# Modulation products with 32 equal moving columns, two more dummies and 48 no-ops, in a fused adaLN attention and MLP kernel

## The chip, the cores and the metric

One core of one Trainium2 chip. The time is the device's time of one execution in microseconds (us), median over the runs given with it; lower is better. Each execution also has a *span*, from its first to its last recorded instruction. The time reaches further: it runs on after the span's end, and "tail" below is the time less the span of the same execution. A ratio of two kernels is the mean time of one kernel's runs over that of the other's of the same rounds, so it is not quite the ratio of the medians.

## The reference

```python
def reference(A_x, A_k_cache, A_v_cache, A_wq, A_wo, B_x, B_w1, B_w2, c, w_mod):
    ...                                     # A: 2048x512, 32 heads of 128, last 512 keys; B: 512-1792-512 with relu
    mod = (_silu(c) @ w_mod).reshape(c.shape[0], 6, 1, -1)
    sa, ca, ga, sb, cb, gb = (mod[:, 0].copy(), ...)
    h = _layernorm(x, axis=-1) * (1 + ca) + sa
    x = x + ga * _A_ref(h, A_k_cache, A_v_cache, A_wq, A_wo)
    h = _layernorm(x, axis=-1) * (1 + cb) + sb
    x = x + gb * _B_ref(h, B_w1, B_w2)
    return x
```

The change touches `sa` and `ca`, the shift and scale of the first normalization: eight column vectors of 128, each a sum of four products of a 128x128 block of `w_mod` with a 128-vector of silu(c).

## The kernel before: the parts that matter

```python
def mm(out_ap, lhsT, rhs, start, stop, reads, bk, signal): ...      # one matmul on TensorE, with waits and signal
def warm(n, gate=(), bk=7):                                          # dummies: 128x512 products of ones, result unused
    for i in range(n):
        mm(bank[bk], ones[:, :], ones[:, 0:1].to_broadcast([P, QB]), True, True, [R_ones] + list(gate), [bk], i == n - 1)

def mod_cols_mm(which, bk):          # 32 products: cc = 4 parts of the weights, each landing by itself; sl, c2 = 8 columns
    ...
    mm(bank[bk][:, col:col + 1], wm[sl][:, cc, c2 * P:(c2 + 1) * P], sc_bf[:, cc:cc + 1], ...)
# [cut]
    ln_tposes(1, TB[0])              # transposes of the normalized rows, 4 per tile
    warm(2, bk=1)
    ln_norm(2)
    mod_half(0, 0, DVE)              # scale and shift of the transposed rows, halves of the block
    mod_half(0, 2, ACT)
    ln_tposes(2, TB[1])
    ln_tposes(3, TB[1])
    mod_half(0, 1, DVE)
    mod_half(0, 3, ACT)
    q_half(0, 0, CC_ORDER, QBK)      # first query products
```

The program ends in a branch. A flag computed from the data says whether the fast path's assumptions held; if not, everything is computed again by a general path, which is never run with these inputs:

```python
                def rerun():
                    kb.emit(stream, e, n_ops)        # the rest of the fast path
                    ...
                    gkb.emit(general[name], e)       # the general path
                if name == "pe":
                    with e.If(v == 128):
                        last_part()                  # TensorE: the side that runs stands first,
                    with e.Else():
                        rerun()                      # then the one that doesn't; a jump leads over it to the end
                else:
                    with e.If(v != 128):
                        rerun()
                    with e.Else():
                        last_part()
```

## Time and profile before

| | before |
|---|---|
| time, median of 6 runs (lowest to highest) | 560.22 us (559.86 to 560.32) |
| profiled execution: time, span | 560.87, 559.0 us |
| TensorE busy | 553.9 us, 99% of the span |
| last part of the modulation weights landed | 8.82 us |
| first score product | 11.65 us |

How it is read is part of the prediction below.

```profile
q8 instruction: 33, 0.54, 0.4%
q14 instruction: 19, 0.16, 0.1%
```

```profile
554.07 1.73 PE L1374 MATMUL psO<-wmw,wq 128*128 128x128 bf16 x28
...
556.16 0.29 DVE L1754 TENSOR_TENSOR PT<-PT,x 128x128 bf16<-128x128 f32 x1
```

TensorE's last product ends at 555.8; VectorE finishes the last rows at 556.45, and the transfer of the output and the last barrier fill the span to 559.0. The two instruction queues fetch the program itself: q8 in packets of 16 KB, which is 256 instructions of 64 bytes (four instructions more lengthen the built program by 256 bytes). The page counts 4139 products and as many weight loads of TensorE, 8278 instructions, which need 33 such packets and are more than those of all other engines together; so q8 is TensorE's.

### The profile page before, as it was taken

To read this page: it belongs to the slowest core of one execution; us is meant where nothing else is said; L and a number is where in the kernel's file an instruction comes from. 1 tells how busy PE (TensorE), PEld (TensorE's weight loads), DVE (VectorE), ACT (ScalarE), POOL (GpSimd) and SP (SyncE) were. 2 spreads that over 40 slices of the span, in tenths; PEclk is the share of its full clock that TensorE was granted. 3 is DMA by queue.
4 is the path that set the end of the run, shared out by engine and by line. 5 is a ranking of instruction groups with operands and counts; after the bars stand their busy time and mean duration, and the time that the engine had idled before them with its cause. 6 is when DMAs were issued, how large, how long until landed. Compare 5 with 4: busy or idle time off the path is not lost.

```text
span 559.0 us, 9759 instructions
## 1 busy us (share of the span) xinstructions
PE 553.9 (99%) x4139; PEld 316.6 (57%) x4139; DVE 254.9 (46%) x556; ACT 349.4 (63%) x455; POOL 52.7 (9%) x50
## 2 busy tenths in 40 slices
PE   8999999999999999999999999999999999999997
PEld 4665555555555555555555555555555554444444
DVE  5555555553546544335445443333354438322134
ACT  5986666666666666666666666666666644432500
POOL 2000022004400000033000000332000000000000
PEclk9999999999999999999999999999999999999999
DMA  9999763422224244353353312121123110200001
GB/s 234 296 196 185 136 166 42 114 43 73 38 41 74 39 84 106 61 130 58 96 95 57 76 40 39 39 38 38 39 39 76 39 29 0 50 28 21 21 29 48
DMA packets 113356, 42.66 MB, mean 76 GB/s; under 512 B 93976, under 2 KB 112152, under 8 KB 113304
## 3 DMA queue, kind: packets, MB, share of 16 engines
q1 hardware_dynamic: 112584, 41.08, 35.5%
q10 hardware_dynamic: 720, 0.89, 0.5%
q8 instruction: 33, 0.54, 0.4%
q14 instruction: 19, 0.16, 0.1%
HBM read 18.35 MB, written 2.10 MB: 37 GB/s over the span
## 4 chain that ended last, share of the span: by engine, by line
PE 98%; DMA 1%; SPq 0%; DVE 0%; issue 0%
PE psS L1374 29%; PE psO L1374 27%; PE psQ L1374 23%; PE psW L1374 20%; DMA wmw<-in_w_mod_dram 1%; SPq L1303 0%; PE psS L1377 0%; PE psO L1377 0%; DVE PT L1752 0%; DVE PT L1754 0%; PE psW L1377 0%
## 5 line engine op out<-in xcount | busy, mean ns | idle before, releaser
L1498 ACT ACTIVATE PT<-psS 128x1024 bf16<-128x1024 f32 x254 | 260.4, 1027 | 127.0 <-PE psS L1374 126.9
L1374 PE MATMUL psS<-qT,kT 128*128 128x512 bf16 (+1 forms) x516 | 151.8, 377 | 0.1
L1374 PEld LDWEIGHTS psO<-v,PT 128*128 128x128 bf16 x2048 | 126.6, 98 | 30.2
L1374 PE MATMUL psO<-v,PT 128*128 128x129 bf16 x2048 | 137.0, 220 | 0.0
L1374 PE MATMUL psW<-wo,oT 128*128 128x512 bf16 x512 | 130.6, 379 | 0.0
L1374 PE MATMUL psQ<-hT,wq 128*128 128x512 bf16 (+1 forms) x508 | 129.6, 377 | 0.0
L1508 DVE RECIPROCAL rinv<-psO 128x4 f32<-128x4 f32 x128 | 23.3, 182 | 225.3 <-PE psO L1374 225.3
L1509 DVE TENSOR_TENSOR o<-psO,rinv 128x512 bf16<-128x512 f32 x128 | 88.5, 691 | 4.7 <-DVE rinv L1508 0.3
L1374 PEld LDWEIGHTS psS<-qT,kT 128*128 128x128 bf16 x516 | 50.0, 98 | 58.7 <-issue 0.4
L1374 PEld LDWEIGHTS psQ<-hT,wq 128*128 128x128 bf16 x508 | 49.7, 98 | 59.0 <-ACT hT L1641 0.2
L1490 ACT ACTIVATE qT<-psQ 128x512 bf16<-128x512 f32 x125 | 73.9, 591 | 0.0
L1741 ACT ACTIVATE wq<-psS 128x512 bf16<-128x512 f32 x56 | 33.4, 597 | 49.1 <-PE psS L1374 49.1
L1374 PEld LDWEIGHTS psW<-wo,oT 128*128 128x128 bf16 x512 | 45.0, 98 | 32.9 <-DVE acc L1531 1.2
L1531 DVE TENSOR_TENSOR acc<-psW,acc 128x512 f32<-128x512 f32 x48 | 33.2, 691 | 6.7 <-PE psW L1374 6.7
L1374 PE MATMUL psO<-wmw,wq 128*128 128x512 bf16 (+1 forms) x168 | 32.9, 352 | 0.0
L1534 POOL TENSOR_TENSOR acc<-acc,gaf 128x512 f32<-128x512 f32 x12 | 15.6, 1301 | 146.9 <-DVE acc L1531 139.8
L1390 POOL TENSOR_TENSOR rstd<-rstd,cst 128x4 f32<-128x4 f32 x7 | 7.2, 1027 | 216.6 <-DVE rstd L1389 216.6
L1752 DVE TENSOR_TENSOR PT<-psO,gbf 128x512 f32<-128x512 f32 (+1 forms) x12 | 7.5, 624 | 40.4 <-PE psO L1374 40.4
L1374 PE MATMUL psS<-h2T,wmw 128*128 128x512 bf16 x112 | 25.3, 379 | 0.0
L1374 PEld LDWEIGHTS psO<-wmw,wq 128*128 128x128 bf16 x168 | 15.4, 98 | 16.5
L1374 PE MATMUL psS<-hT,wmw 128*128 128x512 bf16 x112 | 24.5, 379 | 0.0
L1384 DVE BATCH_NORM_STATS2 st<-x 128x6 f32<-128x512 bf16 x31 | 21.1, 680 | 3.7 <-DMA x<-in_A_x_dram 3.7
(93 smaller groups left out, 197.1 us busy)
## 6 DMA issues: line engine op xcount, KB each, us to landing
wo<-in_A_wo_dram SPq DMA_DIRECT2D x4, 1024.0 KB, 5.9
wq<-in_A_wq_dram SPq DMA_DIRECT2D x7, 512.0 KB, 4.5
wmw<-in_B_w_dram SPq DMA_DIRECT2D x14, 256.0 KB, 3.1
wmw<-in_w_mod_dram SPq DMA_DIRECT2D x4, 512.0 KB, 5.0
oT<-o SPq DMA_TRANSPOSE x128, 2.4
out_dram<-PT SPq DMA_DIRECT2D x15, 128.0 KB, 1.7
x<-in_A_x_dram SPq DMA_DIRECT2D x3, 512.0 KB, 4.3
v<-in_A_v_cache_dram SPq DMA_DIRECT2D x8, 128.0 KB, 4.5
```

Of the source, the lines that this page charges most:

```text
L1374: kb.op(PE, lambda e: e.matmul(out_ap, lhsT, rhs, start=start, stop=stop), reads=reads, group_writes=[R_b[k] for k in bk], signal=signal)
L1384: kb.op(DVE, lambda e: e.bn_stats(st[:, t, :], x_sb[:, t, :]), reads=[R_x[t]], writes=[R_st[t]])
L1390: kb.op(POOL, lambda e: e.tensor_tensor(rstd[:, sl], rstd[:, sl], cst[:, 0:1].to_broadcast([P, hi - lo]), op=ALU.pow), reads=R_rstd[sl] + ...
L1490: kb.op(ACT, lambda e: e.activation(qT[u % NQT][:, :], bank[bk], ACTF.Copy), reads=[R_b[bk]], writes=[R_qT[u % NQT]])
L1498: kb.op(ACT, lambda e: e.activation(PT[u % NPT][:, pr * 2:pr * 2 + 2, :], s_ps[pr][:, :, :], ACTF.Exp, scale=scale), reads=[R_b[pr * 2], R ...
L1508: kb.op(DVE, lambda e: e.reciprocal(rinv[:, u, :], o_ps[:, :, P]), reads=[R_b[5], R_b[6]], writes=[R_rinv])
L1509: kb.op(DVE, lambda e: e.tensor_tensor(o_sb[u % NOS][:, :, :], o_ps[:, :, 0:P], rinv[:, u, :].unsqueeze(2).to_broadcast([P, TPB, P]), op=A ...
L1531: kb.op(DVE, lambda e: e.tensor_tensor(acc[:, tl, :], bank[WBK], acc[:, tl, :], op=ALU.add), reads=[R_b[WBK], R_acc[tl]], writes=[R_acc[tl]])
L1534: kb.op(eng, lambda e: e.tensor_tensor(acc[:, tl, :], acc[:, tl, :], gaf[:, :], op=ALU.mult), reads=[R_acc[tl], R_ga], writes=[R_acc[tl]])
L1741: kb.op(ACT, lambda e: e.activation(h1T[b % 2][:, fc, :], bank[bk], ACTF.Relu), reads=[R_b[bk]], writes=[R_h1[b % 2][fc]], pre=all_events( ...
L1752: kb.op(DVE, lambda e: e.tensor_tensor(yt[i][:, c0:c1], bank[bk][:, c0:c1], gbf[:, c0:c1], op=ALU.mult), reads=[R_b[bk], R_gb], writes=[R_ ...
```

## The change

The intent, as far as it can be read from the code: keep TensorE looking busy while it waits for the modulation weights (32 columns in place of one, two more dummies), so that its clock is not taken down; and move the end of TensorE's program by 48 no-ops that are never run.

```diff
+    NR = 32
@@ mod_cols_mm
-                        bank[bk][:, col:col + 1], wm[sl][:, cc, c2 * P:(c2 + 1) * P], sc_bf[:, cc:cc + 1],
+                        bank[bk][:, col * NR:(col + 1) * NR], wm[sl][:, cc, c2 * P:(c2 + 1) * P], sc_bf[:, cc:cc + 1].to_broadcast([P, NR]),
@@ mod_cols_evac
-        ... bank[bk][:, :2 * DC] ...
+        ... bank[bk][:, :2 * DC * NR].rearrange("p (c r) -> p c r", r=NR)[:, :, 0] ...
@@
     ln_tposes(1, TB[0])
-    warm(2, bk=1)
+    warm(3, bk=1)
@@
     ln_tposes(3, TB[1])
+    warm(1, bk=1)
@@ rerun
                     gkb.emit(general[name], e)
+                    if name == "pe":
+                        for _ in range(48):
+                            e.nop()
```

More of the change, by code (lines that the diff above doesn't have):

```diff
@@ L1439, in mod_cols_evac @@
         mo, r = which * 2 * DC, (R_moda, R_modb)[which]
-        kb.op(DVE, lambda e: e.tensor_tensor(modc[:, mo:mo + 2 * DC], bank[bk][:, :2 * DC], m01[:, :], op=ALU.add), reads=[R_b[bk], R_m01], writes=[r])
+        kb.op(DVE, lambda e: e.tensor_tensor(modc[:, mo:mo + 2 * DC], bank[bk][:, :2 * DC * NR].rearrange("p (c r) -> p c r", r=NR)[:, :, 0], m01[:, :], op=ALU.add), reads=[R_b[bk], R_m01], writes=[r])
     def mod_part(sl, cc):
```

## The prediction

> **What bounds the kernel now.** I read four views, from wide to narrow. First the page: which engine is busy, and whether evenly.
>
> ```profile
> span 559.0 us, 9759 instructions
> PE 553.9 (99%) x4139; PEld 316.6 (57%) x4139; DVE 254.9 (46%) x556; ACT 349.4 (63%) x455; POOL 52.7 (9%) x50
> ...
> PE   8999999999999999999999999999999999999997
> ```
>
> TensorE is busy in every slice; only the first and the last slice show a gap. A busy TensorE is not by itself a bound, so the second view is one long stretch, from the first score product to the start of the last product:
>
> ```profile
> 11.65:555.58 543.93, 543.93 (x4065) 311.84 (x4065) 248.05 (x534) 343.21 (x440) 49.58 (x35) 1.00 0.35 73
> ```
>
> The stretch is 543.93 us long and its matmuls fill 543.93 us. Nothing in it waits for another engine or a transfer, so whatever moves its start moves the end by the same amount. The third view, the list of all waits of TensorE's products, agrees: two lines, both before 9 us.
>
> ```profile
> PE psW L1374 <- DVE ones L1574: 1.1, 1, 1.1
> PE psQ L1374 <- DMA wmw<-in_w_mod_dram: 0.6, 2, 0.4
> ```
>
> The change is in these first 12 us, so the fourth view is the timeline of TensorE there (start, length, engine, line, operation, operands, count, idle time before), and of ScalarE behind it:
>
> ```profile
> 6.13 1.40 PE L1374 MATMUL psW<-ones 128*128 128x512 bf16 x4
> 7.37 0.34 PE L1374 MATMUL psQ<-sc_bf,wmw 128*128 128x1 bf16 x8
> 8.11 0.55 PE L1374 MATMUL psQ<-sc_bf,wmw 128*128 128x1 bf16 x16 [0.40 <-DMA wmw<-in_w_mod_dram]
> 8.87 0.35 PE L1374 MATMUL psQ<-sc_bf,wmw 128*128 128x1 bf16 x8 [0.21 <-DMA wmw<-in_w_mod_dram]
> 9.08 0.61 PE L1377 MATMUL psS<-ident,xn 128*128 128x128 bf16 x8
> 9.53 0.60 PE L1374 MATMUL psS<-ones 128*128 128x512 bf16 x2
> 9.96 0.27 PE L1377 MATMUL psO<-ident,xn 128*128 128x128 bf16 x2
> ...
> 10.40 0.68 PE L1374 MATMUL psQ<-hT,wq 128*128 128x256 bf16 x4
> 10.92 0.60 PE L1374 MATMUL psO<-hT,wq 128*128 128x256 bf16 x4
> 11.65 0.60 PE L1374 MATMUL psS<-qT,kT 128*128 128x256 bf16 x4
> ```
>
> ```profile
> 9.73 1.02 ACT L1641 ACTIVATE hT<-psS,modc 128x256 bf16<-128x256 bf16 x2 [0.61 <-PE psS L1377]
> 10.64 0.56 ACT L1641 ACTIVATE hT<-psW,modc 128x256 bf16<-128x256 bf16 x1
> 11.12 0.38 ACT L1623 ACTIVATE qT<-psQ 128x256 bf16<-128x256 f32 x1
> 11.56 0.38 ACT L1623 ACTIVATE qT<-psO 128x256 bf16<-128x256 f32 x1
> ```
>
> The reader is to see a chain: the last part of the modulation weights lands and the last eight products start (8.87), then transposes (9.08), dummies (9.53), transposes of the other half (9.96), the query products of two heads (10.40, 10.92), the first head's copy on ScalarE (11.12), the first scores (11.65), and from there the gapless stretch.
>
> **What the Trainium skill says.** (1) "TensorE: Matmul & The Clock Gate", section "Wait — 56ns, not 53.3ns?": start to start is N / 2.4 GHz plus about 2.5 ns once warm, and never below about 25 ns, with N = 32 named as standing at that floor. The trace agrees where it can: in the group of 16 products with one column, (0.55 - 0.16) / 15 = 26 ns each; two dummies of 512 columns take 0.60 us, less one length of 0.38 that is 0.22 apart. No product with 32 columns is in this trace. (2) The same page, section "Part 1: The HAM clock gate": the array runs at half rate until about 3.4 us of activity and falls back after an idle window. The first ten dummies lie 0.43 apart (4.45 us less the last one's 0.59, over 9), those after 9.5 us 0.22, and nothing later is slow; so in this execution the clock came up before the modulation products and never fell. (3) "PSUM — Partial Sum Buffer", section "The four PSUM rules": the first product of a group clears the written marks of the whole bank, so only the first of the 32 products needs the flag. That holds for one column per group and for 32 alike (8 x 32 = 256 of 512 columns), so I expect a correct result. (4) "Runtime: NRT & Kernel Launch", section "Instruction fetch mechanics": instructions come in blocks of 256[...]. It bears on the no-ops; no line above shows a cost of it.
>
> **The change part by part.** *32 columns in place of one.* 32 products stay 32 products. By (1) their distance stays at the floor of 25 ns. 24 of them lie ahead of the landing that lets the last eight go at 8.87, so they cost nothing. For the last eight I allow 0 to 2 ns each and 13 ns for the last one's 31 extra columns (an estimate, 31 / 2.4 GHz, from the same section): at most 0.03 us, and I take 0.01. The addition behind them on VectorE reads eight numbers as before, 32 apart; it is ready 0.3 us before its users, who wait for the transposes, so it is hidden.
>
> *Third dummy at 9.53.* Before, the transposes of the second half start at 9.96, when the second dummy has streamed its 512 columns. Their operand had been ready since 9.75 (VectorE's normalization). So they are gated by the dummies, and a third one costs its full 0.216 us: 10.18.
>
> *New dummy behind the transposes.* It stands between the last transpose and the first query product, and costs another 0.216 us on TensorE: the first query product moves from 10.40 to 10.40 + 0.43 = 10.84.
>
> *What other engines give back.* The first four query products take 0.68 us where the next four of the same shape take 0.60: the fourth waited some 0.07 to 0.08 us for ScalarE, whose second result is ready at 10.75 and does not move, as it depends on the first transposes. After the change TensorE arrives there at about 11.16, so that wait is gone: 0.43 - 0.07 = 0.36 us. The gap ahead of the scores, 0.29 us, gives back nothing: the copy at 11.12 starts 0.04 us after the fourth product ends (10.80 + 0.28), and the scores wait for this copy, so the gap moves along. ScalarE's conversion at 10.64 depends on the moved transposes and shifts to about 10.83; it takes some 0.46 us from start to start there, so ScalarE is free at about 11.29, before the copy's new start at 11.48. The scores start at 11.65 + 0.36 = 12.01.
>
> *The no-ops.* In the built program of the changed kernel they are not there: TensorE's instructions grew by four (two dummies, each a weight load and a product), and the branch that is not run has the same number of instructions in both kernels. They wait for nothing and signal nothing, and the build drops them. Even if kept they would stand where TensorE never runs, behind a jump taken after its last product. Cost 0.
>
> *Sum.* 0.01 + 0.216 + 0.216 - 0.07 = 0.37 us at the start of a stretch without slack, so +0.37 us at the end: 560.22 + 0.37 = 560.6 us, 0.07% more.
>
> **The rivals.** *The dummies fill idle time and cost nothing.* For it: TensorE does stand still 0.07 and 0.29 us in this window. Against it: the second gap follows from TensorE's own products through ScalarE. It would give 560.2 us.
>
> *The clock gate, which is what the change seems meant for.* Products with one column, with landings waited for between them, look nearly idle; if the clock fell back in some executions, a window of 3.4 us at half rate would cost up to 1.7 us, and 32 columns and two dummies could prevent it. Against it: in the profiled execution the matmuls behind the products are fast, and the runs lie within 0.46 us (559.86 to 560.32), too close for a loss that comes and goes. For it: the profiled execution took 560.87, so something of half a microsecond does vary. If the median gains from it: 559.3 to 560.
>
> *32 columns are not at the floor.* If a weight load and 32 streamed columns add up, each of the last eight products takes 10 to 15 ns more: +0.1 us, 560.7.
>
> *Code position.* Four more instructions ahead of the branch move everything behind by 256 bytes; if a block boundary fell between, one more fetch of about 1 us could show at the end, where TensorE has been done for 3 us anyway. I give it 2 in 100: 561.5.
>
> **Range and chances.** The mechanism gives +0.3 to +0.5. The larger doubt is what varies between executions and programs, about half a microsecond either way by the four times known. So 559.8 to 561.2 us, with 560.6 in the middle. Two per cent is 11 us; no rival comes near it, so the chance of staying within 2% is 0.98, and 0.01 is left for each side.
>
> **What would show it right or wrong.** Right: products with 32 columns 25 to 27 ns apart; three dummies from 9.53, the second half's transposes at 10.18, the first query product at 10.84, no wait at the fourth, first scores at 12.01 (all plus or minus 0.05 and relative to the last landing of the modulation weights); then a gapless stretch of the same 543.9 us. Wrong: scores at 11.65 (dummies hidden), products over 35 ns apart, slow matmuls after 7 us in either kernel, or a last landing of the weights moved by more than 0.3 us, which would hide the effect of the dummies in either direction.

## The result, and the profile after

| | before | changed |
|---|---|---|
| time, median of 6 runs | 560.22 us (559.86 to 560.32) | 561.38 us (560.68 to 561.92) |
| ratio, 95% interval | | 1.002 (1.0007 to 1.0033) |
| span, median | 558.3 us (9 executions of the first round of experiments) | 558.5 us (6 executions) |
| tail, lowest to highest | 1.78 to 1.91 us (the same 9) | 2.28 to 3.22 us |

The changed kernel is slower by 1.16 us, three times the predicted 0.37, and lies just outside the predicted range. The span explains hardly any of it: 0.2 us. The tail explains 1.1 us (median 2.88 against 1.81). The time went to a place that no view of the span shows.

The timeline of TensorE's start in the changed kernel (line numbers are one higher):

```profile
7.06 1.06 PE L1375 MATMUL psQ<-sc_bf,wmw 128*128 128x32 bf16 x32
8.39 0.72 PE L1378 MATMUL psS<-ident,xn 128*128 128x128 bf16 x8 [0.27 <-DVE xn L1396]
9.17 0.60 PE L1375 MATMUL psS<-ones 128*128 128x512 bf16 x2
9.60 0.27 PE L1378 MATMUL psO<-ident,xn 128*128 128x128 bf16 x2
...
10.05 0.38 PE L1375 MATMUL psS<-ones 128*128 128x512 bf16 x1
10.26 0.60 PE L1375 MATMUL psQ<-hT,wq 128*128 128x256 bf16 x4
10.70 0.60 PE L1375 MATMUL psO<-hT,wq 128*128 128x256 bf16 x4
11.43 0.60 PE L1375 MATMUL psS<-qT,kT 128*128 128x256 bf16 x4
```

One of the three dummies is missing from the records (there is a hole of one dummy's length ahead of 9.17). The first four query products take 0.60 us as the next four do: the wait at the fourth is gone, as predicted. But everything is earlier than predicted, because the weights landed at 7.71 us in this execution and not at 8.82. The transposes now wait for VectorE's normalization, as the first one's idle time says. The stretch behind is the same as before to a hundredth:

```profile
11.43:555.36 543.93, 540.08 (x3992) 311.85 (x4065) 248.14 (x533) 343.25 (x440) 49.56 (x35) 1.00 0.35 73
```

543.93 us again, with the same 4065 weight loads. (TensorE has 3992 product records for 4065 weight loads: 73 are missing, and they, not idle time, explain the 540.08.)

### The profile page after: what moved, and what is told of

Read it like the earlier page. It is cut to its first block, busy times and chain, and to the rows that moved or that the text cites. A ratio compares the mean times of both kernels' runs of the same rounds, so it can differ in the third digit from the quotient of the medians.

```text
span 558.8 us, 9689 instructions
## 1 busy us (share of the span) xinstructions
PE 550.1 (98%) x4067; PEld 316.6 (57%) x4141; DVE 255.0 (46%) x556; ACT 349.7 (63%) x455; POOL 52.7 (9%) x50
## 4 chain that ended last, share of the span: by engine, by line
PE 97%; issue 1%; DVE 1%; DMA 1%
PE psS L1375 29%; PE psO L1375 27%; PE psQ L1375 22%; PE psW L1375 19%; DMA x<-in_A_x_dram 1%; DVE st L1385 0%; PE psS L1378 0%; DVE mv L1386 0%; PE psO L1378 0%; DVE xn L1396 0%; DVE rstd L1594 0%; DVE PT L1754 0%; DVE PT L1756 0%; DVE tmp L1425 0%; DVE sc_bf L1426 0%
## 5 line engine op out<-in xcount | busy, mean ns | idle before, releaser
L1375 PE MATMUL psW<-wo,oT 128*128 128x512 bf16 x452 | 118.1, 379 | 3.2
```

Source lines behind the costliest of these rows:

```text
L1375: kb.op(PE, lambda e: e.matmul(out_ap, lhsT, rhs, start=start, stop=stop), reads=reads, group_writes=[R_b[k] for k in bk], signal=signal)
```

## The experiments

Theories after the result. *Position*: the rival of the prediction that had 2 chances in 100. Four more instructions of TensorE move the end of its program, and something in the tail pays for it. *Start*: the dummies cost what they were predicted to, and the rest is noise. *Clock*: 32 columns or dummies keep the clock up.

### Parts alone, and four instructions that never run

`a_nops`: the kernel before, with the 48 no-ops only (the last part of the diff above).

> The kernel before with the 48 no-ops alone. Position theory (the time behind the last recorded instruction grows with the place of TensorE's program end) and also the theory of the start: 560.2 us, the same as before within 0.2, because the built program has no byte more than before. If the no-ops did survive on the chip's side they would move the end by 48 instructions, and the position theory would allow another tail (time less span): 1 us more or less.

`b_cols`: with the 32 columns only (the first three parts).

> The kernel before with 32 moving columns alone. TensorE's program has the same length as before. Position theory: tail as before, about 1.9 us, time 560.2. Theory of the start: products 25 to 27 ns apart, time +0.0 to +0.1. Clock theory (columns keep the clock up in some executions): time below before by 0.3 or more.

`c_dummies`: with the two dummies only.

> The kernel before with the two dummies alone: four TensorE instructions more. Position theory: the tail grows by about 1 us, as in the changed kernel (2.3 to 3.2 us there against 1.9), time 561.2 to 561.5. Theory of the start: only the span grows, by 0.37 at an equal landing of the weights, time 560.6.

`d_four`: with four instructions in the path that is not run:

```diff
                     gkb.emit(general[name], e)
+                    if name == "pe":
+                        for _ in range(6):
+                            e.wait_ge(meet, len(fast))     # six waits, which the build packs into four instructions
```

> The kernel before with four TensorE instructions more at the end of the path that is never run, nothing else: what is executed is the same, only the place of the program's end moves by 256 bytes. Position theory: tail +1 us, time 561.2. Theory of the start, or a tail that varies by itself: 560.2, tail as before.

| run | TensorE instructions more | time | ratio (95%) | span | tails |
|---|---|---|---|---|---|
| before, same rounds | 0 | 560.11 | | 558.3 | 1.78 to 1.91 |
| a_nops | 0 | 560.20 | 0.9999 (0.9985 to 1.0012) | 558.4 | 1.80 to 1.93 |
| b_cols | 0 | 560.18 | 1.0002 (0.9989 to 1.0016) | 558.4 | 1.76 to 1.87 |
| c_dummies | 4 | 561.77 | 1.0025 (1.0011 to 1.0039) | 558.7 | 2.36 to 3.21 |
| d_four | 4 | 561.44 | 1.0017 (1.0004 to 1.0031) | 558.4 | 2.35 to 3.29 |

Times and spans are medians of five (before: nine), in us. `d_four` executes exactly what the kernel before executes and is 1.3 us slower, all but 0.1 of it in the tail. That settles the larger part: the position theory holds, and the columns and the no-ops alone leave time, span and tail as they were (their ratios are good to 0.7 us). `c_dummies` shows both effects one upon the other: the long tail, and a span 0.3 to 0.4 us longer than that of all others in the table.

### The no-ops made real, and other lengths

The no-ops do nothing because they are not in the built program. (`a_nops` has the length of the kernel before.) `e_real48` is the changed kernel with instructions in their place that the build keeps:

```diff
-                        for _ in range(48):
-                            e.nop()
+                        for _ in range(94):
+                            e.wait_ge(meet, len(fast))     # 94 waits, 48 instructions
```

> The changed kernel with its 48 no-ops made real: 94 waits that the build packs into 48 instructions more than the changed kernel, so TensorE's end lies 52 instructions behind that of the kernel before. Block theory (what counts is where the end of TensorE's program lies in a fetched block of 16 KB, and a block border behind the end costs a fetch in the tail): the border may now lie ahead of the tail, then no second fetch, tail 1.9 or about 1 us less, time 559.6 to 560.6. Length theory (any lengthening costs the microsecond): tail 2.3 to 3.2 as in the changed kernel, 561.4. Spans of both 558.5 to 558.8 (the dummies' 0.3 stay).

`f_plus2`, `f_plus52`, `f_plus128`: `d_four` with 2, 102 and 254 waits, so 2, 52 and 128 instructions.

> The kernel before with two instructions more at the end of the path that is not run. Block theory: a step, so either 560.1 (tail 1.9) or 561.4 (tail 2.3 to 3.2), not between. A cost per instruction: half of the four's, 560.7.

> The kernel before with 52 instructions more there, no dummies and single columns. Block theory: the same tail as the run with real no-ops, span 558.4, so 0.3 us less than that run. Length theory: 561.4.

> The kernel before with 128 instructions more there, half a block. Block theory: the border lies ahead of the tail, the fetch of 16 KB after the last barrier (at 559.3 in the kernel before) is gone, tail no more than 1.9 and possibly about 1.0, time 559.2 to 560.2. Length theory: 561.4 or more.

`f_plus260`, `f_plus16` and `f_plus36` followed, and after them `f_plus3` and `f_plus8`, made in the same way.

> The kernel before with 260 instructions more at the end of the path that is not run, which is the four of the slow case and one block of 256. Block theory: the place within a block is that of the slow case, so the tail is long again, 2.3 to 3.2 us, time about 561.4. If instead the absolute length or something finer than a block counts: tail 1.8 to 1.9, time 560.2.

> 16 more. It looks for the far side of the slow window, known so far as: 2 fast, 4 slow, 52 fast. A border crossed by the few instructions of the program's end: fast again (tail 1.8 to 1.9). A border crossed by a longer sequence behind it: slow (2.3 to 3.2).

> 36 more, the same question nearer to 52. Short sequence: tail 1.8 to 1.9; a sequence of more than 32 instructions: 2.3 to 3.2. A slow place every 32 instructions: slow at 36 and fast at 16.

> The kernel before with three instructions more in the path that is not run. Known: 2 fast, 4 slow, 16 fast, 260 slow. Block theory with a short sequence: either tail, 1.8 to 1.9 or 2.3 to 3.2, nothing between; with 8 it bounds the width of the slow window.

> Eight more, the other side of the window. If the sequence at the program's end that must not straddle a block border is only a few instructions long: fast, tail 1.8 to 1.9. If it is six or more instructions long: slow, 2.3 to 3.2.

| run | instructions more | time | span | tails |
|---|---|---|---|---|
| before, all rounds (36 executions) | 0 | 560.01 to 560.19 | 558.2 to 558.4 | 1.74 to 1.93 |
| f_plus2 | 2 | 560.17 | 558.3 | 1.76 to 1.87 |
| f_plus3 | 3 | 560.98 | 558.6 | 2.25 to 3.15 |
| d_four | 4 | 561.44 | 558.4 | 2.35 to 3.29 |
| f_plus8 | 8 | 561.75 | 558.3 | 3.27 to 3.45 |
| f_plus16 | 16 | 560.00 | 558.2 | 1.80 to 1.81 |
| f_plus36 | 36 | 560.36 | 558.5 | 1.78 to 1.86 |
| f_plus52 | 52 | 560.28 | 558.4 | 1.81 to 1.92 |
| e_real48 (with dummies and columns) | 52 | 560.57 | 558.8 | 1.77 to 1.85 |
| f_plus128 | 128 | 560.34 | 558.5 | 1.77 to 1.91 |
| f_plus260 | 260 | 561.60 | 558.55 | 2.29 to 3.29 |

(For before: the lowest and highest of the medians. 3 to 5 runs of the others.) The tails fall into two groups with nothing between 1.93 and 2.25. Slow are 3, 4 and 8 instructions, and 260, which is 4 and one block of 256. So it is a window less than 14 instructions wide that comes again 256 instructions later: neither the length of the program nor what is executed counts, but where its end lies. A fetched block has just 256 instructions, which fits; but the lengths tried would fit a repeat every 64 or 128 as well, so the block as the period is argued and not shown. Two runs also part the place of the end from the length of the jump to it. In `c_dummies` the branch and the end both move by four, so the jump is as long as before, and the tail is long; in `g_nodummies` below the jump is four longer and the end stands where it was, and the tail is short. Expectations of mine failed on the way: that `e_real48` or half a block more would take a fetch out of the tail. The fetch is still there, and `f_plus128` has the tail of before. A cost of each added instruction is out as well, though within the window the tail seems to grow from 3 (median 2.38) to 8 (3.35; three runs each).

`e_real48` is what the change presumably was when it was made: its end lies outside the window. Its tail is that of before, and its time, 560.57, is 0.5 us above the 560.08 of the kernel before in the same rounds (ratio 1.0006, 0.9992 to 1.002; the mean of before holds one execution that lost its clock, see below), all of it in the span. With 48 real instructions the tail is short and with the 48 no-ops it is long: so the no-ops are not there on the chip either. It also gives the cleanest view of the dummies, because its profiled execution and that of `d_four` had the same start, both with transposes at 8.54 waiting for VectorE. First `d_four` (two dummies), then `e_real48` (three and one):

```profile
8.54 0.72 PE L1377 MATMUL psS<-ident,xn 128*128 128x128 bf16 x8 [0.38 <-DVE xn L1395]
...
9.53 0.27 PE L1377 MATMUL psO<-ident,xn 128*128 128x128 bf16 x2
...
9.97 0.68 PE L1374 MATMUL psQ<-hT,wq 128*128 128x256 bf16 x4
...
11.22 0.60 PE L1374 MATMUL psS<-qT,kT 128*128 128x256 bf16 x4
```

```profile
8.54 0.72 PE L1378 MATMUL psS<-ident,xn 128*128 128x128 bf16 x8 [0.36 <-DVE xn L1396]
...
9.76 0.27 PE L1378 MATMUL psO<-ident,xn 128*128 128x128 bf16 x2
...
10.41 0.60 PE L1375 MATMUL psQ<-hT,wq 128*128 128x256 bf16 x4
...
11.58 0.60 PE L1375 MATMUL psS<-qT,kT 128*128 128x256 bf16 x4
```

The second half's transposes move by 0.23, the query products by 0.44 and shrink by 0.08, the scores move by 0.36: the four steps of the prediction, of 0.22, 0.43, 0.07 and 0.36. (One of the three dummies is missing from these records too; `c_dummies` has all three, from 9.07 on.)

### The branch turned round

What of the position costs: the place in the block, or the jump that leads there? `h_swap4` writes TensorE's branch as the other engines have theirs, so the side that runs stands last and runs into the end without a jump. TensorE's program has the same total length as that of `d_four`.

```diff
-                if name == "pe":
-                    with e.If(v == 128):
-                        last_part()
-                    with e.Else():
-                        rerun()
-                else:
-                    with e.If(v != 128):
-                        ...
+                with e.If(v != 128):
+                    rerun()                  # with eight waits for TensorE at its end, to have the length of d_four
+                with e.Else():
+                    last_part()
```

> The kernel before with the two sides of TensorE's branch exchanged, so that the path that is run stands last and no jump leads over the other one at the end, and with the same four instructions more in total as the slow case. If the long tail needs the jump to the end (its target fetched alone, the next block not yet there): tail 1.8 to 1.9, and the fetch at about 555.5 is gone; the branch in mid-run may cost TensorE up to 2 us. If the place of the end within a block is enough: tail 2.3 to 3.2.

Time 560.20 (before in the same rounds 560.01, ratio 1.0000, 0.9983 to 1.0016), span 558.4, tails 1.77 to 1.81. The short tail at a length that is slow with the jump. The branch in mid-run, for which I had allowed up to 2 us, shows as a wait of 0.2 us in the profile. The trace's records of TensorE's instruction queue agree (start of each fetch of 16 KB from 555 us on, and the end of the span; these records are not in the page's views):

```
              span ends   TensorE's fetches
before          559.0     556.17, 559.27
d_four          558.6     555.22, 558.77
f_plus128       558.4     555.60, 558.72
h_swap4         558.4     none (the last one was at 530.38)
```

With the jump, one block is fetched as TensorE leaves its last product, and another one behind the end of the span; without it there is neither. So at this length the jump is needed for the loss; other lengths without it were not tried.

The instruction records, also outside the views, show what the jump costs within the span. TensorE's last instruction before the final barrier (a drain) starts 2.3 to 2.8 us after its last product has ended, in every profile with the jump, fast or slow, and only 0.18 to 0.36 us before that of SyncE, the last engine to come (558.56 and 558.74 in the kernel before). In `h_swap4` it starts at 554.63, ahead of the last product's end. So the jump eats up nearly all the time by which TensorE is done early.

What the fetches do not show is why one place is slow. The second one is there in fast and slow places alike, 0.13 to 0.88 us behind the span's end in fast ones and 0.13 to 0.67 in slow ones, and TensorE's queue has 34 packets in every run with the jump. The long tail does leave a mark in the other instruction queue, q14: in five of the six slow profiles it fetches once more 2.75 us or later behind the span's end, where in the fast ones nothing comes after 1.90. `f_plus8`, with the longest tail, has no such record. That the last few instructions straddle a border, and TensorE must wait for the second block at a point where the others wait for it, fits a window of some ten instructions, but it is argued and not shown.

### No dummies at that place

`g_nodummies`: the kernel before with the `warm(2, bk=1)` taken out, and four instructions added to the path that is not run, so that the length is that of before.

> The kernel before without its two dummies there, with four instructions more in the path that is not run so that TensorE's program has the length of before. Theory of the start, the other way round (a dummy costs its 0.216 us where transposes follow it without a wait): span down by 0.2 to 0.4, time 559.7 to 559.9, tail 1.8 to 1.9. If the dummies are hidden or keep the clock up: 560.1 or more, with slow matmuls behind 9 us in the second case.

Time 560.23 (before in the same rounds 560.19, ratio 0.9993, 0.9976 to 1.001), span 558.4 like before, tails 1.76 to 1.90. My expectation failed: taking two dummies away gains nothing that is clear of noise, while adding two costs 0.36. The profile of the run says why:

```profile
8.64 0.72 PE L1377 MATMUL psS<-ident,xn 128*128 128x128 bf16 x8
9.49 0.29 PE L1377 MATMUL psO<-ident,xn 128*128 128x128 bf16 x2
...
9.96 0.80 PE L1374 MATMUL psQ<-hT,wq 128*128 128x256 bf16 x4
...
10.47 0.10 PEld L1374 LDWEIGHTS psQ<-hT,wq 128*128 128x128 bf16 x1 [0.19 <-ACT hT L1641]
```

The transposes of the second half start at 9.49, though the first ones are issued by 9.2: they now wait for VectorE's rows. And the query products take 0.80 us instead of 0.68, as the last line says: the fourth one's weight load waits for the rows that ScalarE scales. It starts 1.83 us after the first transposes, here (8.64 to 10.47) as in `d_four`, which has two dummies (8.54 to 10.37). This path goes from the first transposes through ScalarE and past the dummies, so taking them away cannot shorten it. The prediction had seen this wait, of 0.07 us in the kernel before; my expectation forgot it. The two old dummies lie in time that TensorE would wait through anyway. The first extra one no longer does.

### An execution in which the clock fell

The profiled execution of `f_plus36` was one of six, out of the 108 executions whose span is known (including the changed kernel's), with a span of 559.7 to 560.6 us at a mean clock of 0.997. Its stretches, with the granted clock as the third number from the right:

```profile
5.00:8.67 3.67, 3.01 (x41) 1.41 (x40) 3.28 (x13) 2.46 (x9) 2.05 (x4) 1.00 1.22 263
8.67:12.08 3.41, 3.19 (x26) 2.61 (x25) 1.91 (x7) 1.75 (x4) 0.00 (x0) 0.50 1.06 260
12.08:15.00 2.92, 2.80 (x22) 1.91 (x21) 1.28 (x5) 1.85 (x4) 0.00 (x0) 1.00 1.16 316
```

The clock is at half from 8.67 to 12.08 us and the span is some 1.6 us longer. So the loss that the change seems meant to prevent is real. Whether the change prevents it is open: all six were among the 87 executions with single columns and no added dummies; none was among the 21 with columns or added dummies. That says little. All six ran in the rounds of one chip, where 5 of 56 executions had columns or added dummies; drawn at random from those 56, the six would miss these five in more than half of all cases.

## Why the prediction was right and wrong, point by point

- **The bound.** Right. A stretch without slack follows the first scores, 543.93 us long before and after.
- **32 columns stay at the floor.** Right. In the records of single products they are 25 ns apart, as one column is, and last 176 ns instead of 163: the 13 ns of the estimate. `b_cols` is at 1.0002.
- **The dummies: 0.216 + 0.216 - 0.07.** Right, at equal start: 0.36 between `d_four` and `e_real48`, and 0.3 to 0.4 between the median spans of `c_dummies` and of the kernels without added dummies in its rounds.
- **No later landing.** The prediction took the landing at 8.82 from one profile and named a move by more than 0.3 us as what would make it wrong. It moved, to 7.71 after, and between 7.50 and 8.59 in the profiled experiments. That shifts where the chain starts, in either kernel, and hides the dummies if two single profiles are compared.
- **The no-ops.** Right that the build drops them. Wrong was the sentence that they would cost nothing even if kept: kept, they are worth about 1 us, as they move the end out of the slow window (median tail 1.79 in `e_real48`, 2.88 in the changed kernel).
- **Code position, the step that failed.** The prediction counted four more instructions, and said that a fetch at a block border would fall where TensorE "has been done for 3 us anyway", with 2 chances in 100. Those 3 us are no cover. With the jump, TensorE comes to the last barrier only 0.18 to 0.36 us ahead of the last engine, in every profile, and the loss is behind the last barrier, after the span, where no recorded work overlaps it. Nor is it one more fetch: TensorE's queue makes 34 in fast and slow places. Why the place matters stays open. `d_four` shows the term by itself: +1.2 us in the tail, where the prediction had 0. With it the sum comes near what was measured, 1.16: 1.1 for the tail, and 0.2 in the median span where the start was to cost 0.37 and the landings vary by more than that.
- **The clock.** The prediction saw a rival and took the close runs as speaking against it. The loss exists, in 6 of 87 executions, too seldom to move a median.

## What to carry to other kernels

Keep the time and the span apart: when the time moves and the span doesn't, look behind the last instruction and not at the engines. An edit that adds a few instructions to one engine moves everything behind them in its program; here that alone was worth more than the edit. So test an edit of some tenths of a microsecond against a control of the same length in a path that is not run, make sure that padding survives the build, or let the path that runs stand last so that no jump leads to the end (tried here at one length). A dummy is free only as long as it lies in a wait: count the wait before adding one more.

## What the Trainium skill lacked or had wrong

- "Runtime: NRT & Kernel Launch", section "Instruction fetch mechanics", says that a taken branch out of the window forces a fetch. It lacks that the place of the jump's target at the end of a program counts, and comes again after 256 instructions: 3, 4, 8 and 260 instructions more made the tail 2.25 to 3.45 us, 0, 2, 16, 36, 52 and 128 left it at 1.74 to 1.93, and without the jump it was 1.77 to 1.81 at the slow length.
- The same page, section "The ~15µs preamble/postamble breakdown", gives the stages behind the kernel one figure each. Here all that the time holds behind the last record, the tail, is 1.7 to 1.9 us or 2.3 to 3.5 us, by the program's layout alone.
- "TensorE: Matmul & The Clock Gate", section "HAM oscillation — how this bites in real kernels", ties the fall of the clock to gaps of more than some 3.4 us. In `f_plus36` it fell at 8.67 us with no gap of TensorE over 0.6 us in the 3.4 us before, which held dummies until 6.9 and then products of one column. The page's next section, "A second HAM failure mode: psum-queue depth-cycling", does know a fall from many short pauses, in another kind of kernel; products of one column are not named.
- The same page, section "Wait — 56ns, not 53.3ns?", gives the floor of about 25 ns but not whether it holds with a weight load ahead of each product. Here it does: 25 ns from start to start, at 1 column and at 32.
- No page says that a no-op without a wait or a signal may be left out by the build: 48 of them added no byte to the program here.
